# Two sliding-window attention problems on one core: the first loads on one queue, Q weights in halves, second x quarter in two pieces, Q of all blocks ahead of K, first V chain of that quarter unpinned

## The chip, the core and the metric

The kernel runs on one core of a Trainium2 chip. The time is device microseconds of that core for one execution, as a median of several runs. The engines named below are TensorE (PE, with its weight loads as PEld), VectorE (DVE), ScalarE (ACT), GpSimd (POOL) and SyncE (SP), whose queue issues most of the loads.

## The reference

Two independent problems, A and B, each with x of 2048 x 1024, and the results side by side. All inputs are bf16.

```python
def ref(x, wqkv, wo):
    B, S, D = x.shape                      # 1, 2048, 1024
    H = 32; Dh = D // H; W = 256
    qkv = (x @ wqkv).reshape(B, S, 3, H, Dh).transpose(2, 0, 3, 1, 4)
    q, k, v = qkv[0], qkv[1], qkv[2]
    scores = jnp.einsum("bhqd,bhkd->bhqk", q, k) * (Dh ** -0.5)
    idx = jnp.arange(S)
    mask = (idx[:, None] - idx[None, :] >= 0) & (idx[:, None] - idx[None, :] < W)
    p = softmax(jnp.where(mask, scores, -1e9))
    o = jnp.einsum("bhqk,bhkd->bhqd", p, v)
    return o.transpose(0, 2, 1, 3).reshape(B, S, D) @ wo
```

Each query sees the 256 keys up to its own position, so the scores form a band.

## The kernel before

**Tiling.** x is held transposed in quarters of 512 rows (`xT[(problem, quarter)]`, 128 partitions x 8 column tiles x 512). The weights of Q and K come for four heads at a time (a group `g`, 8 groups to a problem, `wqk[g]`), the weights of V for eight heads (`wv[m]`). A *Q or K chain* is eight matmuls of 512 columns that make one group's Q or K for one quarter; a *V chain* is sixteen matmuls of 256 columns for two blocks of 128 rows; an *output chain* is eight matmuls of 512 columns. Each chain ends with a copy out of its bank (`pp`) by ScalarE or VectorE (lines 216 and 218). There are two such banks.

**Sessions.** The band is cut into units of 64 queries by 128 keys; eight units make a score set. A session (`session`, line numbers around 528 to 562) issues the score matmuls of a set, two exponentials on ScalarE and the masks on GpSimd. Between two sessions the kernel's own planner puts in chains: `emit_all` and `forced` take them from a list sorted by the latest session at which they are needed (`late`), each with an earliest session (`early`); `level` works out how much of this work goes in now. Once probabilities times V are due, the chains up to the next session are issued in a split form (four matmuls of 32 columns of weights, line 197, in place of one of 128, line 193).

**The start.** The first quarter of x is loaded as four blocks of 128 rows (`xrow`, line 647) and turned by TensorE (`flip`, eight transposes a block, line 680, then a copy each by ScalarE and VectorE, line 682). `first(which, a)` does Q (`which` 0) or K (1) for one block `a`, eight matmuls of 128 columns. The later quarters come by transposing loads (`load_x`, line 154). The order of the loads on SyncE's queue is that of the code: blocks 0 and 1, K weights, blocks 2 and 3, V weights, second quarter, weights of group 1, third quarter, second V weights, fourth quarter; the Q weights of group 0 are issued by ScalarE. Until data is there TensorE multiplies a blank tile (`keep_warm`, line 667), six times before the first flip and twice after it. On TensorE the order is: flip 0, two blanks, flip 1, Q on block 0, K on block 0, flip 2, Q on block 1, flip 3, K on block 1, Q on blocks 2 and 3, K on blocks 2 and 3, one V chain, then the first session.

Of the kernel before, what the change touches and what calls it, by code (L numbers as in the profile page):

```python
# [10 lines left out]
I32 = mybir.dt.int32  # L11
# [7 lines left out]
P = 128  # L19
# [6 lines left out]
QB = 4  # L26
# [8 lines left out]
NS_MM = 216.0  # L35
# [4 lines left out]
FREE = 10 ** 6  # L40
# [43 lines left out]
def _fast_path(ctx, tc, cfg, problems, outs, consts, certify, osbp, ps_acc, ps_proj, last_stores):  # L84
# [57 lines left out]
    xT, wqk, wv, wo_sb, vts, oTs, qks, pts = {}, {}, {}, {}, {}, {}, {}, {}  # L142
    edges, diags = {}, {}

    top = once.tile([P, 256], I32, name="top")
    nc.vector.memset(top[:], 0)
    blank = top[:].bitcast(BF16)

# [3 lines left out]
    def load_x(pi, k, a=0, n=QB, c0=0, c1=CT):  # L152
        lo, hi = a * P, (a + n) * P
        nc.sync.dma_start_transpose(
            out=xT[(pi, k)][:, c0:c1, lo:hi],
            in_=problems[pi][0][k * 512 + lo:k * 512 + hi, c0 * P:c1 * P])
# [7 lines left out]
    def load_wqk(g, which, queue, lo=0, hi=CT):  # L164
        pi, t = divmod(g, T)
        queue.dma_start(out=wqk[g][:, lo:hi, which, :],
                        in_=wsrc(pi)[:, lo:hi, which, t * P:(t + 1) * P])
# [219 lines left out]
    def landed(*key):  # L387
        return arrival.get(key, 0)
# [18 lines left out]
    for m in range(NM):  # L407
        for b in range(0, NB, 512 // (VG * P)):
            k = b // QB
            early = max(0, landed("x", m * VG // T, k), landed("wv", m))  # L410
            if m > 1:
                early = max(early, pv_time(VG * (m - 1) - 1, min(2 * k + 2, NP - 1)) + 1)
            late = pv_time(VG * m, b // 2) if m or k else 1
            chains.append(_Chain(early, late, v_steps(m, b), dense=True))
# [19 lines left out]
            fixed[d] += NS_PV * (10 if p else 6)  # L434

    current = []

    def start_chain(now, left):
        able = [n for n, c in enumerate(chains) if c.early <= now]
        if not able:  # L440
            return False
        pick = able[0]
        want = whole[0] == (left > 900.0)
        if chains[pick].late > now + 1 and chains[pick].dense != want:
            pick = next((n for n in able if chains[n].dense == want
                         and chains[n].late <= now + REACH), pick)
        current.extend(chains.pop(pick).steps)
        return True

    def run_side():  # L450
# [18 lines left out]
    def emit_all(now, budget):  # L469
        emit(now, budget)  # L470
        second_half()

    def forced(now):
        while any(c.late <= now for c in chains):
            assert current or any(c.early <= now for c in chains), [
                (c.early, c.late, now, c.size) for c in chains if c.late <= now]
            emit(now, sum(ns for ns, _ in current) or chains[0].size)
        if any(c.late <= now + 1 for c in chains):
            emit(now, sum(ns for ns, _ in current))
# [162 lines left out]
    new_wqk(0)  # L642
    new_wv(0)
    xrow = [rows[:, 2 * a:2 * a + 2, :].rearrange("p t n -> p (t n)") for a in range(QB)]
    load_wqk(0, 0, nc.scalar)
    for a in range(QB):
        nc.sync.dma_start(out=xrow[a], in_=problems[0][0][a * P:(a + 1) * P, :])
        if a == 1:
            load_wqk(0, 1, nc.sync)
    load_wv(0, 0, CT, nc.sync)  # L650
    new_x(0, 1)
    load_x(0, 1)
    new_wqk(1)
    for which in range(2):
        load_wqk(1, which, nc.sync)
# [8 lines left out]

    def keep_warm(n):
        for _ in range(n):
            nc.tensor.matmul(warm[:], lhsT=blank[:, 0:P], rhs=blank[:, 0:512], start=True, stop=True)

    keep_warm(6)
    half = CT // 2  # L670
    held = [{}, {}]

# [11 lines left out]
    def first(which, a):  # L684
        for _, f in qk_steps(0, which, 0, a * P, (a + 1) * P, held[which], last=a == QB - 1):
            f()

    with tc.tile_pool(name="ps_flip", bufs=4, space=PSUM) as ps_flip:
        flip(0)
        keep_warm(2)  # L690
        flip(1)
        first(0, 0)
        first(1, 0)
        flip(2)
        first(0, 1)
        flip(3)
        for which, a in ((1, 1), (0, 2), (0, 3), (1, 2), (1, 3)):
            first(which, a)
    emit(0, chains[0].size)

# [2 lines left out]
    for now in range(END):  # L703
        forced(now)
        settle(now)
        whole[0] = not (due and due[0][0] <= now)
        session(now)
        while due and due[0][0] <= now:
            _, pg, pk = due.pop(0)
            finish_norm(1)  # L710
            pv(pg, pk)
        if not whole[0]:
            finish_norm(1)
        if due and due[0][0] == now + 1:
            finish_norm()
        while edges_due and edges_due[0][0] <= now:
            edge(*edges_due.pop(0)[1:])
        emit_all(now, level(now) - fixed[now])
    while edges_due:
        edge(*edges_due.pop(0)[1:])  # L720
    while due:
# [140 lines left out]
@with_exitstack  # L862
def kernel(
    ctx: ExitStack,
    tc: tile.TileContext,
    A_x: bass.AP,
    A_wqkv: bass.AP,
    A_wo: bass.AP,
    B_x: bass.AP,
    B_wqkv: bass.AP,  # L870
    B_wo: bass.AP,
    out: bass.AP,
):
    nc = tc.nc
    S, D = A_x.shape[-2], A_x.shape[-1]
    cfg = _Cfg(S, D)
    problems = [(x.flatten_outer_dims(), wqkv, wo)
                for (x, wqkv, wo) in ((A_x, A_wqkv, A_wo), (B_x, B_wqkv, B_wo))]
    of = out.flatten_outer_dims()
    outs = [of[:, pi * D:(pi + 1) * D] for pi in range(len(problems))]  # L880

    cpool = ctx.enter_context(tc.tile_pool(name="consts", bufs=1))
    ones = cpool.tile([P, 2, 32], BF16, name="ones")
    nc.vector.memset(ones[:], 0.0)
    nc.vector.memset(ones[:, 0, 0:16], 1.0)
    nc.vector.memset(ones[:, 1, 16:32], 1.0)
    ones1 = cpool.tile([P, 1], F32, name="ones1")
    nc.vector.memset(ones1[:], 1.0)
    pm = cpool.tile([P, 1], F32, name="pm")
    okp = cpool.tile([P, 1], F32, name="okp")  # L890
    unsafe_i = cpool.tile([1, 1], I32, name="unsafe_i")
    ident = cpool.tile([P, P], BF16, name="ident")
    nc.gpsimd.memset(ident[:], 0.0)
    nc.gpsimd.affine_select(out=ident[:], in_=ident[:], pattern=[[-1, P]],
                            compare_op=ALU.not_equal, fill=1.0, base=0, channel_multiplier=1)
    consts = {"ones": ones, "ident": ident}

    def reduce_bits(top):
        seen = top[:, 0:8]
        nc.vector.tensor_single_scalar(out=seen, in_=seen, scalar=OUT_OF_RANGE, op=ALU.bitwise_and)  # L900
        nc.vector.tensor_reduce(out=pm[:], in_=seen, axis=AX.X, op=ALU.max)
        nc.vector.tensor_scalar(out=okp[:], in0=pm[:], scalar1=0.5, scalar2=None,
                                op0=ALU.is_lt)

    def decide(pool):
        csum = pool.tile([P, 512], F32, name="pp")
        nc.tensor.matmul(csum[0:1, 0:1], lhsT=ones1[:], rhs=okp[:], start=True, stop=True)
        nc.vector.tensor_scalar(out=unsafe_i[:], in0=csum[0:1, 0:1], scalar1=float(P) - 0.5,
                                scalar2=None, op0=ALU.is_lt)

    last_stores = []
    osbp = ctx.enter_context(tc.tile_pool(name="osb", bufs=4))
    ps_acc = ctx.enter_context(tc.tile_pool(name="ps_acc", bufs=2, space=PSUM))
    ps_proj = ctx.enter_context(tc.tile_pool(name="ps_proj", bufs=2, space=PSUM))
    with tc.manual_schedule():
        with ExitStack() as fctx:
            _fast_path(fctx, tc, cfg, problems, outs, consts, [reduce_bits, decide], osbp, ps_acc,
                       ps_proj, last_stores)

    unsafe = nc.values_load(unsafe_i[0:1, 0:1], min_val=0, max_val=1)  # L920

    with tc.If(unsafe > 0, preferred_fallthrough_block=True) as found:
        with ExitStack() as sctx:
            spool = sctx.enter_context(tc.tile_pool(name="s_consts", bufs=1))
            _make_slow_consts(nc, consts, spool)
            for pi, (x, wqkv, wo) in enumerate(problems):
                with ExitStack() as pctx:
                    _slow_problem(pctx, tc, cfg, x, wqkv, wo, outs[pi], consts)
    with found.Else():
        with tc.manual_schedule():  # L930
            for n, (place, pp, lo, hi) in enumerate(last_stores):
                osb = osbp.tile([P, 512], BF16, name="osb")
                copy = nc.scalar.copy if n % 2 == 0 else nc.vector.tensor_copy
                copy(out=osb[:, lo:hi], in_=pp[:, lo:hi])  # L934
                queue = nc.scalar if n >= 2 else nc.sync
                queue.dma_start(out=place, in_=osb[:, lo:hi])
# [30 lines left out]
```

## Time and profile before

| | |
|---|---|
| median of 3 runs | 599.55 us (598.75 to 599.72) |
| profiled execution | 599.05 us, of which the span is 597.3 us |
| TensorE busy | 582.3 us, 97% of the span |
| ScalarE busy | 402.0 us, 67% |
| GpSimd busy | 365.3 us, 61% |
| VectorE busy | 352.6 us, 59% |
| DMA moved | 35.67 MB, of them 6.37 MB in the first 40 us |

The busy share of an engine is taken over the whole span. What a change in the first microseconds is worth is read from the rows of that stretch: when a load was issued, how long it took to land, and which engine waited for it. In the rows, the time in square brackets is the idle time of the engine just before the row, with what ended it. Ends of matmuls are modelled, so the starts are the safer numbers.

### The profile page before, as it was taken

To read this page: it belongs to the slowest core of one execution; us is meant where nothing else is said; L and a number is where in the kernel's file an instruction comes from. 1 tells how busy PE (TensorE), PEld (TensorE's weight loads), DVE (VectorE), ACT (ScalarE), POOL (GpSimd) and SP (SyncE) were. 2 spreads that over 40 slices of the span, in tenths; PEclk is the share of its full clock that TensorE was granted. 3 is DMA by queue.
4 is the path that set the end of the run, shared out by engine and by line. 5 is a ranking of instruction groups with operands and counts; after the bars stand their busy time and mean duration, and the time that the engine had idled before them with its cause. 6 is when DMAs were issued, how large, how long until landed. Compare 5 with 4: busy or idle time off the path is not lost. (4 is left out here: it accounts for less than half of the span.)

```text
span 597.3 us, 31844 instructions
## 1 busy us (share of the span) xinstructions
PE 582.3 (97%) x14155; PEld 360.2 (60%) x14226; DVE 352.6 (59%) x973; ACT 402.0 (67%) x502; POOL 365.3 (61%) x918
## 2 busy tenths in 40 slices
PE   8999999999999999999999999999999999999997
PEld 6666665666557656566656657665556655555443
DVE  1265766676677776774566656666666656666100
ACT  4667777777877877776567767676676776774332
POOL 0658667777777878765466666666667666665000
PEclk9999999999999999999999999999999999999999
DMA  9915110111024103545011100102030030114122
GB/s 243 181 39 145 39 40 3 40 40 38 4 48 101 39 3 57 109 99 130 10 39 39 38 3 20 42 20 74 3 83 20 24 98 13 55 56 135 64 80 74
DMA packets 86815, 35.67 MB, mean 60 GB/s; under 512 B 65552, under 2 KB 86160, under 8 KB 86672
## 3 DMA queue, kind: packets, MB, share of 16 engines
q1 hardware_dynamic: 85344, 33.18, 22.8%
q8 instruction: 113, 1.85, 1.3%
q10 hardware_dynamic: 1328, 0.39, 0.3%
q14 instruction: 30, 0.25, 0.1%
HBM read 17.83 MB, written 8.39 MB: 44 GB/s over the span
## 5 line engine op out<-in xcount | busy, mean ns | idle before, releaser
L538 ACT ACTIVATE pt<-st 128x1024 bf16<-128x1024 f32 x304 | 299.2, 1025 | 86.7 <-PE st L528 40.6
L549 POOL TENSOR_SCALAR_AFFINE_SELECT diag<-pt 128x256 bf16<-128x256 bf16 x512 | 215.5, 446 | 181.9 <-ACT pt L538 171.1
L562 POOL TENSOR_SCALAR_AFFINE_SELECT pt<-pt 128x512 bf16<-128x512 bf16 (+1 forms) x256 | 155.2, 625 | 0.0
L576 DVE TENSOR_TENSOR both<-diag,pt 128x512 bf16<-128x512 bf16 (+1 forms) x256 | 123.0, 520 | 16.5 <-POOL diag L549 9.6
L193 PE MATMUL pp<-xT,wqk 128*128 128x512 bf16 (+1 forms) x538 | 121.7, 360 | 6.5 <-issue 5.2
L197 PE MATMUL pp<-xT,wqk 128*32 128x512 bf16 x1924 | 114.6, 379 | 0.0
L619 DVE STREAM_TRANSPOSE turned<-acc 128x128 f32<-128x128 f32 x128 | 39.8, 311 | 99.0 <-PE acc L609 99.0
L193 PE MATMUL pp<-wv,xT 128*128 128x256 bf16 x756 | 89.8, 273 | 0.0
L193 PEld LDWEIGHTS <-wqk 128*128 128x128 bf16 x591 | 51.5, 98 | 51.1 <-DMA wqk<-in_A_wqkv_dram 0.2
L193 PEld LDWEIGHTS <-xT 128*128 128x128 bf16 x756 | 72.2, 98 | 14.6
L193 PE MATMUL pp<-wo_sb,oT 128*128 128x512 bf16 x323 | 74.0, 379 | 2.0 <-issue 1.3
L528 PEld LDWEIGHTS <-kT 32*64 32x64 bf16 x3904 | 41.1, 103 | 56.3 <-issue 56.2
L197 PEld LDWEIGHTS <-wqk 128*32 128x32 bf16 x1924 | 48.8, 97 | 39.0
L528 PE MATMUL st<-qT,kT 32*64 32x64 bf16 (+4 forms) x3904 | 65.9, 236 | 0.2 <-issue 0.2
L626 DVE STREAM_TRANSPOSE wide<-inv 128x256 f32<-128x256 f32 x128 | 57.0, 445 | 4.3
L193 PEld LDWEIGHTS <-oT 128*128 128x128 bf16 x357 | 33.9, 98 | 38.4 <-issue 0.2
L627 DVE TENSOR_TENSOR oT<-acc,wide 128x256 bf16<-128x256 f32 x128 | 54.3, 424 | 4.5
L216 ACT CAST osb<-pp 128x512 bf16<-128x512 f32 x49 | 28.7, 586 | 39.5 <-PE pp L193 27.0
L609 PE MATMUL acc<-pt,vt 128*32 128x128 bf16 (+2 forms) x1792 | 48.8, 223 | 0.0
L609 PEld LDWEIGHTS <-vt 128*32 128x32 bf16 x2816 | 43.5, 97 | 7.7 <-issue 0.4
L216 ACT CAST qT<-pp 128x512 bf16<-128x512 f32 x52 | 30.5, 587 | 19.2 <-PE pp L197 10.1
L216 ACT CAST vt<-pp 128x512 bf16<-128x512 f32 x45 | 26.4, 588 | 23.2 <-PE pp L193 12.3
(49 smaller groups left out, 421.8 us busy)
## 6 DMA issues: line engine op xcount, KB each, us to landing
out_dram<-osb SPq DMA_DIRECT2D x63, 128.0 KB, 1.9
wqk<-in_B_wqkv_dram SPq DMA_DIRECT2D x32, 128.0 KB, 2.8
wqk<-in_A_wqkv_dram SPq DMA_DIRECT2D x24, 128.0 KB, 2.9
wo_sb<-in_A_wo_dram SPq DMA_DIRECT2D x16, 128.0 KB, 2.6
wv<-in_B_wqkv_dram SPq DMA_DIRECT2D x16, 128.0 KB, 2.5
wo_sb<-in_B_wo_dram SPq DMA_DIRECT2D x16, 128.0 KB, 2.5
oT<-in_A_x_dram SPq DMA_DIRECT2D x4, 256.0 KB, 4.8
wv<-in_A_wqkv_dram SPq DMA_DIRECT2D x2, 512.0 KB, 6.2
```

Of the source, the lines that this page charges most:

```text
L193: nc.tensor.matmul(out[:, lo:hi], lhsT=lhsT, rhs=rhs, start=start, stop=stop, skip_group_check=True)
L197: nc.tensor.matmul(out[c:c + 32, lo:hi], lhsT=lhsT[:, c:c + 32], rhs=rhs, start=start, stop=stop, tile_position=(0, c), skip_group_check=True)
L216: nc.scalar.copy(out=out, in_=in_)
L528: nc.tensor.matmul(scores[c * HALF:(c + 1) * HALF, r, a * HALF:(a + w_) * HALF], lhsT=kT[rows, keys], rhs=qT[rows, q:q + w_ * HALF], start ...
L538: nc.scalar.activation(out=pt[:, lo:lo + 2, :n * HALF], in_=scores[:, lo:lo + 2, :n * HALF], func=ACT.Exp, bias=-SHIFT, scale=cfg.scale)
L549: nc.gpsimd.affine_select(out=diags[(g, p)][:, :, h, lo:lo + HALF], in_=pt[:, :, a * HALF:(a + 1) * HALF], pattern=[[0, 4], [1, HALF]], co ...
L562: nc.gpsimd.affine_select(out=blk, in_=blk, pattern=[[0, 4], [-1, w_ * HALF]], compare_op=ALU.is_gt, fill=0.0, base=-HALF * (us[a][2] - 3) ...
L576: nc.vector.tensor_tensor(out=both[:, :, h, o:o + w_], in0=dg[:, :, h, o:o + w_], in1=pts[t][:, :, a:a + w_], op=ALU.add)
L609: nc.tensor.matmul(acc[32 * r:32 * r + 32, o:o + w_], lhsT=lhsT, rhs=src[:, r, :], start=(x == 0), stop=(x == len(moves) - 1), tile_positi ...
L619: nc.vector.transpose(out=turned[:], in_=acc[:, 2 * P:3 * P])
L626: nc.vector.transpose(out=wide[:], in_=inv[:].unsqueeze(3).to_broadcast([P, 2, QB, 32]))
L627: nc.vector.tensor_tensor(out=oTs[(pi, k)][:, t, (p % 2) * 256:(p % 2 + 1) * 256], in0=acc[:, 0:256], in1=wide[:], op=ALU.mult)
```

## The change

The Q weights of group 0 move from ScalarE's queue to SyncE's, in two halves of four column tiles, between blocks 1 and 2 of x; the K weights go behind block 3. The second quarter of x is loaded in two pieces of 256 rows. On TensorE, Q of all four blocks now comes ahead of K of all four, the two blank matmuls after flip 0 are gone, and the warm-up is ten blank matmuls of 256 columns in place of six of 512. The blank tile is half as wide; the memsets of the constants `ones` and `ones1` move from VectorE to GpSimd. In the planner, the first V chain of the second quarter may start with session 0, session 0 is followed by at least two chains' worth of work, and a chain that is under way is finished in `forced` once its own latest session has come.

```diff
-    top = once.tile([P, 256], I32, name="top")
+    top = once.tile([P, P], I32, name="top")
...
             early = max(0, landed("x", m * VG // T, k), landed("wv", m))
+            if m == 0 and b == QB:
+                early = 0
...
     current = []
+    current_late = [FREE]
...
-        current.extend(chains.pop(pick).steps)
+        chain = chains.pop(pick)
+        current.extend(chain.steps)
+        current_late[0] = chain.late
         return True
...
     def forced(now):
+        if current and current_late[0] <= now:
+            emit(now, sum(ns for ns, _ in current))
...
-    load_wqk(0, 0, nc.scalar)
     for a in range(QB):
         nc.sync.dma_start(out=xrow[a], in_=problems[0][0][a * P:(a + 1) * P, :])
         if a == 1:
-            load_wqk(0, 1, nc.sync)
+            for c in range(0, CT, 4):
+                load_wqk(0, 0, nc.sync, c, c + 4)
+    load_wqk(0, 1, nc.sync)
     load_wv(0, 0, CT, nc.sync)
     new_x(0, 1)
-    load_x(0, 1)
+    for a in range(0, QB, 2):
+        load_x(0, 1, a, 2)
...
-            nc.tensor.matmul(warm[:], lhsT=blank[:, 0:P], rhs=blank[:, 0:512], start=True, stop=True)
-
-    keep_warm(6)
+            nc.tensor.matmul(warm[:, 0:256], lhsT=blank[:, 0:P], rhs=blank[:], start=True, stop=True)
+
+    keep_warm(10)
...
         flip(0)
-        keep_warm(2)
         flip(1)
         first(0, 0)
-        first(1, 0)
         flip(2)
         first(0, 1)
         flip(3)
-        for which, a in ((1, 1), (0, 2), (0, 3), (1, 2), (1, 3)):
+        for which, a in ((0, 2), (0, 3), (1, 0), (1, 1), (1, 2), (1, 3)):
             first(which, a)
...
-        emit_all(now, level(now) - fixed[now])
+        room = level(now) - fixed[now]
+        emit_all(now, room if now else max(room, 2 * NS_MM * CT))
...
-    nc.vector.memset(ones[:], 0.0)
-    nc.vector.memset(ones[:, 0, 0:16], 1.0)
-    nc.vector.memset(ones[:, 1, 16:32], 1.0)
-    nc.vector.memset(ones1[:], 1.0)
...
+    nc.gpsimd.memset(ones[:], 0.0)
+    nc.gpsimd.memset(ones[:, 0, 0:16], 1.0)
+    nc.gpsimd.memset(ones[:, 1, 16:32], 1.0)
+    nc.gpsimd.memset(ones1[:], 1.0)
```

SyncE's queue at the start of the program, before (`oT` is the tile that holds the rows of x before they are turned; x2 after a row counts it twice in a row):

```order
L647 DMA oT<-in_A_x_dram 128x1024 x2
L166 DMA wqk<-in_A_wqkv_dram 128x8x128
L647 DMA oT<-in_A_x_dram 128x1024 x2
L175 DMA wv<-in_A_wqkv_dram 128x8x256
L154 DMA_TRANSPOSE xT<-in_A_x_dram 128x8x512
```

And after:

```order
L653 DMA oT<-in_A_x_dram 128x1024 x2
L166 DMA wqk<-in_A_wqkv_dram 128x4x128 x2
L653 DMA oT<-in_A_x_dram 128x1024 x2
L166 DMA wqk<-in_A_wqkv_dram 128x8x128
L175 DMA wv<-in_A_wqkv_dram 128x8x256
L154 DMA_TRANSPOSE xT<-in_A_x_dram 128x8x256 x2
```

The whole load of weights ahead of the second pair of blocks was K's; now it is Q's in two halves, K's comes after the pair, and the transposing load is in two.

TensorE, at the end of Q on block 0, before (`pp_179` is Q's bank, `pp_188` K's; in brackets what a row waits for, DMAHW being a load):

```order
L193 LDWEIGHTS wqk_123
L193 MATMUL pp_179<-xT_122,wqk_123 128x128
L193 LDWEIGHTS wqk_123 [waits DMAHW3_49]
L193 MATMUL pp_188<-xT_122,wqk_123 128x128 [waits PE_49]
L193 LDWEIGHTS wqk_123
```

And after (`pp_183` is Q's bank):

```order
L193 LDWEIGHTS wqk_123
L193 MATMUL pp_183<-xT_122,wqk_123 128x128
L689 LDWEIGHTS oT_121 [waits DMAHW4_49]
L689 MATMUL turned_192<-ident_63,oT_121 128x128 [waits PE_49]
L689 LDWEIGHTS oT_121
```

K on block 0 stood there and waited for its weights; now the transposes of block 2 follow at once, and all of K comes after Q on block 3.

ScalarE, which copies the banks out between the exponentials, from the end of the start on, before:

```order
L216 CAST qT<-pp 128x512
L216 CAST kT<-pp 128x512
L216 CAST vt<-pp 128x512
L538 ACTIVATE pt<-st 128x1024 x2
L216 CAST qT<-pp 128x512
L538 ACTIVATE pt<-st 128x1024 x2
```

And after:

```order
L216 CAST qT<-pp 128x512
L216 CAST kT<-pp 128x512
L216 CAST vt<-pp 128x512
L545 ACTIVATE pt<-st 128x1024 x2
L216 CAST vt<-pp 128x512
L216 CAST qT<-pp 128x512
L545 ACTIVATE pt<-st 128x1024 x2
```

One more V chain (`vt`) is finished between the first and the second pair of exponentials, ahead of the Q chain on the second quarter.

## Rows read from the trace of the kernel before

**Rows 1.** The page, part 1: busy us (share of the span) x instructions of TensorE.

```profile
PE 582.3 (97%) x14155; PEld 360.2 (60%) x14226; DVE 352.6 (59%) x973; ACT 402.0 (67%) x502; POOL 365.3 (61%) x918
```

**Rows 2.** Windows: stretch, its length, then busy us of each engine (instructions).

```profile
0.00:15.00 15.00, 13.17 (x156) 9.84 (x156) 2.11 (x9) 6.78 (x10) 0.70 (x6) 1.00 1.02 243
15.00:45.00 30.00, 29.52 (x598) 19.30 (x603) 13.40 (x35) 18.82 (x24) 16.90 (x40) 1.00 0.53 109
```

**Rows 3.** Waits of TensorE over the span: us in total, times, longest.

```profile
PE pp L193 <- issue: 6.5, 41, 0.2
```

**Rows 4.** Timeline of the start, TensorE's matmuls: start us, us, engine, line, out<-in.

```profile
1.31 2.74 PE L667 MATMUL pp<-top 128*128 128x512 bf16 x6 [1.31 <-DVE ones L886]
...
3.85 1.01 PE L680 MATMUL turned<-ident,oT 128*128 128x128 bf16 x8
...
4.69 0.59 PE L667 MATMUL pp<-top 128*128 128x512 bf16 x2
...
5.70 0.62 PE L680 MATMUL turned<-ident,oT 128*128 128x128 bf16 x8 [0.41 <-DMA oT<-in_A_x_dram]
...
8.40 0.61 PE L680 MATMUL turned<-ident,oT 128*128 128x128 bf16 x8
...
8.84 2.40 PE L193 MATMUL pp<-xT,wqk 128*128 128x128 bf16 x40
...
11.08 1.91 PE L193 MATMUL pp<-wv,xT 128*128 128x256 bf16 x16
```

**Rows 5.** Timeline of the start, TensorE's weight loads.

```profile
1.72 0.15 PEld L667 LDWEIGHTS <-top 128*128 128x128 bf16 x1 [0.28 <-issue]
...
5.69 0.45 PEld L680 LDWEIGHTS <-oT 128*128 128x128 bf16 x8 [0.90 <-DMA oT<-in_A_x_dram]
...
6.82 0.45 PEld L193 LDWEIGHTS <-wqk 128*128 128x128 bf16 x8 [0.23 <-DMA wqk<-in_A_wqkv_dram]
7.49 0.45 PEld L680 LDWEIGHTS <-oT 128*128 128x128 bf16 x8 [0.23 <-DMA oT<-in_A_x_dram]
...
15.08 0.98 PEld L193 LDWEIGHTS <-wqk 128*128 128x128 bf16 x6 [0.17 <-DMA xT<-in_A_x_dram]
```

**Rows 6.** Timeline of the start, SyncE's queue: start and length of the issues.

```profile
0.80 0.87 SPq L647 DMA_DIRECT2D oT<-in_A_x_dram  x2
...
2.19 1.05 SPq L647 DMA_DIRECT2D oT<-in_A_x_dram  x2
3.29 0.43 SPq L175 DMA_DIRECT2D wv<-in_A_wqkv_dram  x1
3.76 7.63 SPq L154 DMA_TRANSPOSE xT<-in_A_x_dram  x1
```

**Rows 7.** Loads by narrow windows of issue: KB, us from issue to landing.

```profile
wqk<-in_A_wqkv_dram ACTq DMA_DIRECT2D x1, 256.0 KB, 4.1
oT<-in_A_x_dram SPq DMA_DIRECT2D x1, 256.0 KB, 3.0
...
oT<-in_A_x_dram SPq DMA_DIRECT2D x1, 256.0 KB, 5.3
...
wv<-in_A_wqkv_dram SPq DMA_DIRECT2D x1, 512.0 KB, 6.7
...
xT<-in_A_x_dram SPq DMA_TRANSPOSE x1, 11.3
```

**Rows 8.** Timeline of the start, VectorE: its copy of block 3.

```profile
9.04 0.42 DVE L682 COPY xT<-turned 128x512 bf16<-128x512 bf16 x1 [0.47 <-PE turned L680]
```

**Rows 9.** Transposing loads, line 154: length of the issues, ns min/median/max, starts.

```profile
L154 SPq DMA_TRANSPOSE xT<-in_B_x_dram x32: 1194/1222/2661, 175.8 to 278.5; - x32
L154 SPq DMA_TRANSPOSE xT<-in_A_x_dram x3: 5659/6520/7633, 3.8 to 19.0; - x3
```

**Rows 10.** Groups by form: Q and K chains, wide and split; busy us, mean ns.

```profile
L193 PE MATMUL pp<-xT,wqk 128*128 128x512 bf16 x474 | 117.4, 379 | 6.4 <-issue 5.2 <-PE st L528 0.2
L197 PE MATMUL pp<-xT,wqk 128*32 128x512 bf16 x1924 | 114.6, 379 | 0.0
```

## The prediction

> **What bounds the kernel now.** I read the busy shares first, then the stretches, then who waits for whom, and only then the first 16 us row by row. TensorE is busy 582.3 us of a 597.3 us span [rows 1], and from 15 us on it misses only 0.48 us in 30 us [rows 2]. The longest entry in the list of its waits is 6.5 us put down to "issue", in 41 pieces of 0.2 us at most [rows 3]; next to it only the wait of 1.31 us at the very start is over a microsecond long and has an engine for its cause [rows 4]. So the work after the first stretch is a queue of matmuls with hardly a gap, and a change that reorders this queue can win or lose only what is left in gaps. The one stretch with room is 0 to 15 us, where 1.83 us are idle [rows 2]; there the loads set the pace. The reader is to see three things in rows 4 and 5: the weight loads of TensorE wait 0.90 us for block 1 of x, 0.23 for the K weights and 0.23 for block 2, so each starts as its load lands; from block 2 at 7.49 on nothing waits until the V work starts at 11.08; and the last wait for a load, 0.17 us at 15.08, is for the second quarter of x.
>
> The profiled execution took 599.05 us (597.3 us of span and 1.75 us around it); the median of the three runs is 599.55 and they spread from 598.75 to 599.72. I make the sum as a difference and put it on the median too. A difference of under about 0.2% (1.2 us) is what a measurement of this kernel cannot tell from none.
>
> **Part 1: the order of the loads.** Block 0 of x lands at 0.80 + 3.0 = 3.8, block 1 at 5.69, the K weights at 6.82, block 2 at 2.19 + 5.3 = 7.49, the V weights at 3.29 + 6.7 = 9.99; the Q weights, on ScalarE's queue beside the blocks, take 4.1 us and are there before block 1 [rows 5 to 7]. The time to landing grows from 3.0 to 6.7 us down the queue while the issues follow each other in half a microsecond, so I read these landings as a line of data waiting for the same engines, not as a fixed latency. From this, K cost 6.82 - 5.69 = 1.13 us of the line, and a block of x 7.49 - 6.82 = 0.67. After the change the data ahead of block 2 is blocks 0 and 1 and Q, without K. Whether Q runs beside the blocks or between them, block 2 should land 1.13 us earlier, at about 6.35, block 3 at about 7.0, K at about 8.2, and the V weights at 9.99 as before, since the same bytes are ahead of them.
>
> Bounds of that landing. Optimistic: Q beside block 0 had held it back by half of its 1.13 us; block 0 alone lands at 3.25 and block 2 then at 3.25 + 0.67 + 1.13 + 0.67 = 5.72. Pessimistic: landings are tied to issues. Q in halves puts two issues in front of block 2 where K's one stood; at 0.43 us an issue (the V weights' [rows 6]) block 2 is issued at about 2.6 and by the 5.3 us of its row lands at 7.9. I take 6.35, as the growth of the landing times speaks for the line.
>
> The row for block 0, beside the Q load of the other queue, is 3.0 us from issue to landing, and block 2, four loads later, takes 5.3 [rows 7]. [...]
>
> **Part 2: TensorE up to the first V work.** Before, from block 2's landing: its eight transposes and Q on block 1 from 7.49 to 8.40, block 3's transposes to 8.84, then five groups of eight matmuls (2.24 us, 0.45 each) to 11.08 [rows 4, 5]; 3.59 us in all. After the change K on block 0 stands behind block 2 as well, and the order is: transposes of block 2 and Q on block 1 0.91, transposes of block 3 0.44, Q on blocks 2 and 3 0.90, four groups of K 1.79. That adds 0.45. One wait is new: Q on block 3 needs the copies of block 3, the last of which ends at 9.04 + 0.42 = 9.46 [rows 8], 1.06 us after block 3's transposes start at 8.40; only these transposes and one group lie between now, so 1.06 - 0.44 - 0.45 = 0.17 us. Together 3.59 + 0.45 + 0.17 = 4.21, and the V work starts at 6.35 + 4.21 = 10.56 instead of 11.08: **0.52 us earlier**. With the bounds of part 1 it starts at 9.99 (the V weights hold it there) to 12.1: a gain of 1.09 to a loss of 1.0. The K weights (8.2) are wanted at 8.77 and hold nothing up.
>
> **Part 3: warm-up and memsets.** The warm-up falls from 8 matmuls of 512 columns to 10 of 256, none between the flips. The two removed there took 0.59 us at 4.69 [rows 4], and block 1 came later anyway, so removing them frees nothing. The memset of the blank tile is first on VectorE and half as large; TensorE starts at about 1.1 instead of 1.31, ten matmuls at 0.21 (half of the 0.28 + 0.15 = 0.43 us from one weight load to the next in rows 5) end at about 3.25, and then it waits for block 0. The ones go to GpSimd, which has nothing else to do before the first exponentials. Cost in time: nothing, unless TensorE's clock depends on it (rival 2).
>
> **Part 4: second quarter of x, and the V chain.** Between the first and second score sets the program now has two V chains ahead of the Q chain on the second quarter; the new one needs only the first half of that quarter. The first scores follow the first V chain, at 10.56 + 1.91 = 12.5, take some 0.35 us, and each V chain takes 1.91 [rows 4]; so the first half is wanted at 14.8 and the second at 16.7. Before, the whole landed at 3.76 + 11.3 = 15.06 [rows 6, 7]. It was in line behind the V weights of 9.99, so the first half should be there at about (9.99 + 15.06) / 2 = 12.5. Two pieces cost more issue time: pieces of an eighth take 1.22 us each on the queue against 5.66 us for a whole quarter at best [rows 9], which splits into about 0.6 us a piece and 5.1 us for the data; so 0.6 us more, and the second half lands at 15.1 to 15.7, still ahead of 16.7. The wait of **0.17 us** goes, and the 0.52 us gained ahead of it is not turned into a longer wait there. The third quarter's load begins some 0.6 us later; its first chain stands behind one more V chain of 1.9 us, so its cover grows.
>
> The rest of the order differs up to about the 18th score set and is then the same row for row. The count of wide and split chains moves a little: nine groups fewer of the split 512-column form (114.6 us / 481 groups = 0.238) in favour of the wide one (117.4 us over the 527 in the program = 0.223) [rows 10], 0.13 us less; five V groups more in split form, at the same difference, 0.07 us more. Net **0.06 us** less; its bounds are 0 and 0.13.
>
> **Sum:** 0.52 + 0.17 + 0.06 = 0.75 us less: 599.05 - 0.75 = 598.3 for the profiled execution, 599.55 - 0.75 = **598.8** for the median. That is 0.13%: no change that can be told.
>
> **Rivals.**
> 1. *Landings follow issues.* Then part 1 is at its pessimistic end: V at 12.1, and 1.0 - 0.17 - 0.06 = 0.8 us slower, 600.3. Against it: the landing times that grow from 3.0 to 6.7 us. Chance 0.10.
> 2. *TensorE's clock rises late (the slower side).* [...] After the change there is a gap at 3.25 and another before block 2. A 128-column matmul costs 0.107 at the low level and 0.056 at the high one. If the low level holds over block 1, Q on block 0 (its weights landed by 5.69) ends at 6.55, 0.2 us past block 2's landing, and each further matmul loses 0.05. Up to about 8.0 this is 14 matmuls: 0.7 + 0.2 - 0.75, so 599.7, no change. Slower by 1.2 us needs 35 such matmuls, a low clock up to 10.3; with all 72 up to the V work it is 3.6 + 0.2 - 0.75 = 3.0 us, 602.6. [...] Chance 0.12 for the mild end, 0.05 for the slow one.
> 3. *The second half of the quarter comes late.* It costs from 16.7 on; 1.2 us slower needs a landing past 18.6, 3.5 us later than the whole before. Chance 0.03, 0.02 of it slower.
> 4. *More is won.* With block 2 at 5.72 the V work starts at 9.99 and the gain is 1.09 + 0.17 + 0.13 = 1.39 us, 598.15. Chance 0.12 for over 1.2 us.
>
> **How the numbers follow.** Forecast (a gain of 0.4 to 1.2 us) 0.58; rivals 0.10, 0.17, 0.03, 0.12. Faster 0.12; slower 0.05 + 0.02 = 0.07; within 0.2% the other 0.81. The range runs from rival 4's 598.15 to rival 1's 600.3, each with a little for the spread of runs: 597.9 to 600.4. The slow end of rival 2 and most of rival 3 lie outside.
>
> **What would show it.** Block 2's transposes at 6.2 to 6.6 and the first V matmul at 10.3 to 10.8 bear out parts 1 and 2; block 2 at 7.8 shows rival 1. Eight transposes of block 1 or 2 in about 0.85 us show rival 2. No wait of TensorE on the second quarter bears out part 4, a weight load that waits there for its second half shows rival 3. The forecast is wrong if TensorE's idle time after 15 us changes by more than half a microsecond.

## The result, and the profile after

The changed kernel took 603.07 us (median of six, 602.33 to 604.04) against 599.79 us before (median of six executions of the same comparison, 598.75 to 600.12). The ratio is 1.0061, with an interval of 1.0050 to 1.0072: slower by 3.3 us, outside the forecast range. The profiled execution took 603.45 us, with a span of 601.7 us against 597.3.

The start of the changed kernel, TensorE's matmuls and under them two of its weight loads (as rows 4 and 5):

```profile
1.12 2.31 PE L676 MATMUL pp<-top 128*128 128x256 bf16 x10 [1.12 <-DVE top L146]
...
3.57 1.89 PE L689 MATMUL turned<-ident,oT 128*128 128x128 bf16 x16
...
7.47 1.03 PE L689 MATMUL turned<-ident,oT 128*128 128x128 bf16 x8
...
9.15 1.06 PE L689 MATMUL turned<-ident,oT 128*128 128x128 bf16 x8
...
10.01 3.11 PE L193 MATMUL pp<-xT,wqk 128*128 128x128 bf16 x48
...
12.96 1.91 PE L193 MATMUL pp<-wv,xT 128*128 128x256 bf16 x16
...
6.81 0.34 PEld L193 LDWEIGHTS <-wqk 128*128 128x128 bf16 x4 [1.19 <-DMA wqk<-in_A_wqkv_dram]
7.47 0.77 PEld L689 LDWEIGHTS <-oT 128*128 128x128 bf16 x8 [0.32 <-DMA oT<-in_A_x_dram]
```

The V work starts at 12.96 instead of 11.08 [rows 4]: 1.88 us lost. Block 2 lands at 7.47, where it landed before [rows 5], and the second half of Q only at 6.81. The transposes still take 1.03 and 1.06 us for eight, the slower of the two rates in these traces, where they took 0.62 from block 1 on. The record of the granted clock in the two traces agrees: its first entry, with the full share (1.00), begins at 4.67 us before and only at 10.56 us after.

The rest of the loss comes much later. ScalarE's exponentials of the 19th score set and of the last one, in the kernel before:

```profile
79.38 1.94 ACT L538 ACTIVATE pt<-st 128x1024 bf16<-128x1024 f32 x2 [0.58 <-PE st L528]
...
543.01 1.95 ACT L538 ACTIVATE pt<-st 128x1024 bf16<-128x1024 f32 x2
```

And in the changed one:

```profile
81.50 1.94 ACT L545 ACTIVATE pt<-st 128x1024 bf16<-128x1024 f32 x2 [0.58 <-PE st L535]
...
547.57 1.95 ACT L545 ACTIVATE pt<-st 128x1024 bf16<-128x1024 f32 x2
```

At the 19th set the changed kernel is 2.12 us late, at the last one 4.56 us. Between them both kernels issue the same rows in the same order, and still 2.44 us are lost. Where they go is seen in weight loads of split chains, most of them V chains, that wait for nothing the profile names:

```profile
117.88 0.11 PEld L197 LDWEIGHTS <-xT 128*32 128x32 bf16 x6 [0.71 <-issue]
...
130.88 0.10 PEld L197 LDWEIGHTS <-xT 128*32 128x32 bf16 x3 [0.32 <-issue]
...
289.06 1.31 PEld L197 LDWEIGHTS <-xT 128*32 128x32 bf16 x49 [0.81 <-issue]
...
378.76 0.86 PEld L197 LDWEIGHTS <-xT 128*32 128x32 bf16 x32 [1.10 <-issue]
```

In the list of waits these and smaller ones are one line, in the changed kernel and before:

```profile
PEld L197 <- issue: 5.6, 11, 1.1
...
PEld L197 <- issue: 1.8, 3, 1.2
```

Seven of the eleven stand in split V chains, two in split Q or K chains and two in split output chains. Two of the three before are:

```profile
285.02 1.54 PEld L197 LDWEIGHTS <-xT 128*32 128x32 bf16 x59 [1.19 <-issue]
...
374.18 1.10 PEld L197 LDWEIGHTS <-xT 128*32 128x32 bf16 x42 [0.39 <-issue]
```

One trap: TensorE's busy share rose to 99%, and the 6.5 us of "issue" in 41 pieces [rows 3] are absent from this trace. They are back in other kernels' traces (6.3 us in 40 pieces in the first experiment, which is slower than before). Traces that have the entry hold some 70 fewer matmuls than weight loads (14155 and 14226 before [rows 1]); the changed kernel's has 14216 of both. So the entry goes with missing records and was no time to be won.

### The profile page after: what moved, and what is told of

Its sections match the earlier page's. It is cut to its first block, busy times and chain, and to the rows that moved or that the text cites. A ratio compares the mean times of both kernels' runs of the same rounds, so it can differ in the third digit from the quotient of the medians.

```text
span 601.7 us, 31898 instructions
## 1 busy us (share of the span) xinstructions
PE 593.3 (99%) x14216; PEld 363.8 (60%) x14216; DVE 350.9 (58%) x967; ACT 403.1 (67%) x504; POOL 364.5 (61%) x922
## 4 chain that ended last, share of the span: by engine, by line
PE 98%; DMA 1%; issue 0%; SPq 0%; DVE 0%; DVEq 0%
PE pp L193 47%; PE pp L197 28%; PE acc L616 13%; PE st L535 9%; DMA oT<-in_A_x_dram 1%; PE turned L689 0%; PE acc L193 0%; SPq L166 0%; SPq L653 0%; DVE osb L942 0%; DVE unsafe_i L916 0%; PE pp L915 0%; DVEq L942 0%
## 5 line engine op out<-in xcount | busy, mean ns | idle before, releaser
L193 PE MATMUL pp<-xT,wqk 128*128 128x512 bf16 (+1 forms) x600 | 133.1, 366 | 0.9 <-DMA wqk<-in_A_wqkv_dram 0.9
L193 PEld LDWEIGHTS <-wqk 128*128 128x128 bf16 x600 | 53.6, 99 | 53.1 <-DMA wqk<-in_A_wqkv_dram 1.2
L193 PE MATMUL pp<-wo_sb,oT 128*128 128x512 bf16 x341 | 76.7, 379 | 0.2 <-DVE unsafe_i L916 0.2
```

The lines of the kernel that those rows point to most:

```text
L193: nc.tensor.matmul(out[:, lo:hi], lhsT=lhsT, rhs=rhs, start=start, stop=stop, skip_group_check=True)
```

## The experiments

In all but the last, which is a single execution, the kernel before had medians of 599.8 to 600.0 us beside them, and the ratios are to it. Where a blank matmul of one column is added it is of this form, into the scratch bank of the warm-up:

```diff
+    for _ in range(10):
+        nc.tensor.matmul(warm[:, 0:1], lhsT=blank[:, 0:P], rhs=blank[:, 0:1], start=True, stop=True)
```

**The warm-up undone (e1).** The changed kernel with

```diff
-            nc.tensor.matmul(warm[:, 0:256], lhsT=blank[:, 0:P], rhs=blank[:], start=True, stop=True)
-    keep_warm(10)
+            nc.tensor.matmul(warm[:], lhsT=blank[:, 0:P], rhs=blank[:, 0:512], start=True, stop=True)
+    keep_warm(6)
...
         flip(0)
+        keep_warm(2)
```

> The changed kernel with the warm-up of before (six blank matmuls of 512 columns, two more after flip 0). Theory A: in the changed kernel TensorE ran at the low level up to about 10.5 us, because the shorter warm-up let it idle, and that is most of the 1.9 us by which its V work started later (12.96 against 11.08). Then eight transposes take 0.45 us again from block 1 on, the V work starts at about 11.7 (block 2's landing at 7.47 plus 4.21), and the time falls by about 1.3 us, to 601.8. Rival B: the loads set the pace and the clock follows them; then the V work stays at 12.5 to 13.0 and the time at 603.

602.29 us, ratio 1.0034 (1.0021 to 1.0046). Block 1's transposes, block 2's, and the V work:

```profile
4.77 0.61 PE L689 MATMUL turned<-ident,oT 128*128 128x128 bf16 x8
...
7.41 0.62 PE L689 MATMUL turned<-ident,oT 128*128 128x128 bf16 x8 [0.27 <-DMA oT<-in_A_x_dram]
...
11.60 1.91 PE L193 MATMUL pp<-wv,xT 128*128 128x256 bf16 x16
```

The V work is 1.36 us sooner, as theory A said, and the record of the granted clock begins at 3.99 us instead of 10.56. Block 2 lands no earlier (7.41 against 7.47). The median falls by 0.8 of the 1.3 us expected.

**Q back on ScalarE's queue (e2).**

```diff
+    load_wqk(0, 0, nc.scalar)
     for a in range(QB):
...
-            for c in range(0, CT, 4):
-                load_wqk(0, 0, nc.sync, c, c + 4)
```

> The changed kernel with the Q weights whole on ScalarE's queue again, K still behind block 3. Theory B: the two halves of Q on SyncE's own queue held up what stands behind them (second half landed at 6.81, block 2 at 7.47 as before although K was gone from ahead of it). Then Q lands by about 5 us, block 2 at about 6.35, the wait of 0.9 us for Q goes, and with no such gap the clock may rise sooner: V work at 10.6 to 12.3 instead of 12.96, 0.7 to 2.4 us less. Rival A, the warm-up alone: block 2 comes earlier but the transposes still take 0.85 us up to about 10.5, V work at 12.4 or later, 0.6 us less at most.

603.90 us, ratio 1.0060 (1.0043 to 1.0077), but in two groups: 601.28 and 601.67, and four at 603.9 to 604.6. The profiled one is the 601.28: its V work starts at 10.87, block 2's transposes at 6.68 without a wait (0.61 us for eight), and its clock record begins at 4.85. The four longer ones have no trace. By the 1.95 us of e8 below, a low rate that lasts longer would cost most of the difference of 2.2 to 3.3 us; this is an estimate, and no run shows it.

**The planner's edits undone (e3).**

```diff
-            if m == 0 and b == QB:
-                early = 0
...
-        if current and current_late[0] <= now:
-            emit(now, sum(ns for ns, _ in current))
...
-        room = level(now) - fixed[now]
-        emit_all(now, room if now else max(room, 2 * NS_MM * CT))
+        emit_all(now, level(now) - fixed[now])
```

> The changed kernel without its three edits in the planner, so that the first V chain of the second quarter stands where it stood. Theory C: the planner's edits only reorder work that TensorE does anyway and cost nothing by themselves; the time stays within 0.6 us of 603.1. Rival D: the later part of the loss (2.4 us between the 18th score set and the end, where the order of both kernels is the same) comes with the edits, through the shift of TensorE's instruction stream by 20 rows or the other split chains; then the time falls by 1 to 2.4 us.

601.42 us, ratio 1.0020 (1.0008 to 1.0032): 1.65 us back, though the V work still starts at 12.94. Theory C falls: the planner's edits carry about half of the loss.

**The same place in the stream (e4).** Ten blanks of one column behind `keep_warm(10)`.

> The changed kernel with ten more blank matmuls of one column after the warm-up, so that from the 18th score set on every row stands at the same place of TensorE's stream as in the kernel before. Theory E: the stalls put down to issue in the split chains (weight loads of line 197: 5.6 us in 11 pieces in the changed kernel against 1.8 us in 3 before) depend on where in the stream a row stands; then they fall back to about 2 us and the time by 1.5 to 2.4 us, to 601 or 601.5. Rival F: they fall at random, or follow the loads in flight; then they stay between 2 and 6 us at other places and the time does not move by more than 0.6 us.

601.09 us, ratio 1.0016 (1.0006 to 1.0026): 2.0 us back from adding work, with 3.3 us of these stalls instead of 5.6. That is more than theory E's 2 us of stalls, but rival F, which allowed such a sum, did not allow the fall of the time. The V work came at 12.61 in its trace, so some 0.35 of it may be the start's.

**The same in the kernel before (e5).** Ten blanks behind the two after flip 0.

> The kernel before with ten more blank matmuls of one column after the two behind flip 0, where TensorE waits for block 1 anyway, so that all that follows stands 20 rows later in its stream. Theory E (stalls by place in the stream): the start stays as it was within 0.1 us, the V work at 11.1, and the later part changes by stalls at other sessions; the 20 rows go the other way than the changed kernel's, so the sign is not fixed: 0 to 2.5 us more, with stalls put down to issue of 3 to 6 us instead of 1.8. Rival F (at random or by the loads): the same stalls and the same time within 0.4 us.

598.69 us, ratio 0.9979 (0.9968 to 0.9990): faster than both kernels by adding ten blanks. Theory E had expected 0 to 2.5 us more: that the place matters was right, the direction was missed. The V work starts at 10.99, within 0.1 us of before, and no stall of line 197 is left in its trace; one of 0.86 us now stands in a score set (line 528, at 234.9 us).

**The planner's edits alone (e6).** The kernel before with e3's lines put in.

> The kernel before with the three planner edits alone, the loads, the warm-up and the order of Q and K as before; its stream after the 18th score set stands 24 rows earlier. Theory E with a front without loss: V work at 11.1, the wait of 0.17 us for the second quarter stays or goes, and after the 18th score set 1.4 to 2.4 us more than before, with the stalls of the changed kernel at the same sessions (28 and 104 by 0.4 to 0.8 us each): 601 to 602. Rival: the later loss of the changed kernel hangs on its loads or its start; then 599.6, as the kernel before.

603.21 us, ratio 1.0051 (1.0034 to 1.0067): as much as the whole loss of the changed kernel, with the old loads and the old warm-up. Not all of it is the later stretch: in its trace the V work starts at 11.46 (0.38 late) and a weight load near the end waits 0.7 us for the output weights. From the 19th score set to the last it takes 2.5 us more than before. Its stalls:

```profile
116.18 0.10 PEld L197 LDWEIGHTS <-xT 128*32 128x32 bf16 x4 [0.98 <-issue]
...
129.48 0.09 PEld L197 LDWEIGHTS <-xT 128*32 128x32 bf16 x1 [0.63 <-issue]
...
287.65 1.21 PEld L197 LDWEIGHTS <-xT 128*32 128x32 bf16 x47 [0.79 <-issue]
...
377.26 0.77 PEld L197 LDWEIGHTS <-xT 128*32 128x32 bf16 x30 [0.99 <-issue]
```

Here the reader can count. A weight load and its matmul are two rows of the program. The stall near 117 us leaves 6 weight loads before the next score set in the changed kernel and 4 here; that score set begins at row 5325 of TensorE's stream there and at 5321 here. So the stall stands at row 5325 - 12 = 5321 - 8 = **5313** in both. The one near 130 us is row **6081** in both. The one near 287 us leaves 59, 49 and 47 loads of its row in the kernel before, the changed one and this one. The 10 and 12 loads by which these differ are the 20 and 24 rows by which the streams differ there, so it too stands at one row in all three. Counted through the traces, with one row for each of the few wait rows in TensorE's list, that row is **14529**, which is 5313 + 36 times 256 (the 14589 and 19129 in the expectation of e9 do not agree with this count, by which the second is 19137). And the first five of the changed kernel's, rows 2497, 4033, 5313, 6081 and 6849, differ by 6, 5, 3 and 3 times 256.

**All three parts mended (e7).** The edits of e1 and e2 together, and twelve blanks behind the two after flip 0.

> The changed kernel with Q whole on ScalarE's queue, the warm-up of before, and twelve blank matmuls of one column after those behind flip 0, so that the later rows stand where they stood before. Theories A, B and E together: clock at the higher level from about 4.5, block 2 by 6.6, V work at 10.6 to 10.9 in all runs, stalls of 2 to 3.5 us: 599.0 to 600.0, at or a little under the kernel before. If the shift of the stream is not what costs, the later part still loses 1.4 to 2.4 us against before: 601 to 602.

600.15 us, ratio 1.0010 (1.0000 to 1.0021). Block 2's transposes and the V work:

```profile
6.36 0.62 PE L689 MATMUL turned<-ident,oT 128*128 128x128 bf16 x8
...
10.55 1.91 PE L193 MATMUL pp<-wv,xT 128*128 128x256 bf16 x16
```

The start is won (10.55), but it is given back up to the 19th score set: that set comes 0.04 us earlier than before, where the start was 0.53 us earlier. Of the 0.49 us, 0.43 are one stall of the same kind, at 42.8 us in a split V chain.

**The warm-up alone (e8).** The kernel before with the changed warm-up.

> The kernel before with the changed warm-up alone (ten blank matmuls of 256 columns, none behind flip 0, a blank tile half as wide); its stream shifts by 4 rows. Theory A: the clock rises late in some or all runs, since TensorE now waits from about 4.8 to 5.7 for block 1; where it does, each eight transposes or matmuls take 0.85 us up to about 10 and the V work starts at 12.3 to 13.2: 601 to 602, with a spread of 2 us between runs. Rival B (the loads alone): V work at 11.1 and 599.8 within 0.4 us.

601.78 us, ratio 1.0023 (1.0011 to 1.0034): five runs at 600.15 to 600.73, seven at 601.74 to 602.75. In the profiled execution the first eight transposes of block 1 and the V work are

```profile
5.81 1.03 PE L680 MATMUL turned<-ident,oT 128*128 128x128 bf16 x8 [0.87 <-DMA oT<-in_A_x_dram]
...
13.03 1.91 PE L193 MATMUL pp<-wv,xT 128*128 128x256 bf16 x16
```

so the warm-up alone costs 1.95 us at the start of this execution, whose clock record begins only at 10.65 us, and 1.9 us in the median.

**The planner's edits, rows back in place (e9).** e6 with twelve blanks behind the two after flip 0.

> The kernel before with the three planner edits (603.2 us, 3.35 over before) and twelve blank matmuls of one column behind flip 0, where TensorE waits; after the 18th score set every row then stands where it stood before. Theory E: the stalls at rows 5313, 6081 and 6849 of TensorE's stream now fall outside the split V chains and go, those at 14589 and 19129 are those of before; 599.6 to 600.5. If the planner's order itself costs (its other split chains, one V chain more ahead), the time stays at 602.5 to 603.5.

600.66 us, ratio 1.0014 (1.0003 to 1.0026). Twelve blanks take 2.55 of the 3.35 us back. The stalls at rows 5313 and 6081 are gone, but not because these rows left the split V chains, as expected: 16 and 13 loads of such chains still follow them. What differs is that 20 and 27 split loads stand directly ahead of them, where e6 has 32 and 39. The third that was to go, at row 6849, stays (0.60 us). The one at 14529 and the one after it are back where the kernel before had them, with 59 and 42 loads left:

```profile
285.86 1.54 PEld L197 LDWEIGHTS <-xT 128*32 128x32 bf16 x59 [0.78 <-issue]
...
375.26 1.10 PEld L197 LDWEIGHTS <-xT 128*32 128x32 bf16 x42 [0.66 <-issue]
```

**Twenty rows further (e10).** e7 with 22 blanks.

> As the run with Q on ScalarE's queue, the warm-up of before and 12 blank matmuls of one column (600.15 us), but with 22 of them: the later rows stand 20 rows later than before, where the padded kernel before had its 598.7 us. Theory E: V work at 10.55 to 10.7, the stalls of the padded kernel, 598.0 to 598.9, under both kernels. Against it: the stretch up to the 18th score set has another order and its own stalls, up to 0.7 us; then 599.0 to 599.6.

599.76 us, ratio 0.9997 (0.9988 to 1.0006). Short of the hope: the longer row of blanks ends late (V work at 11.20 in its trace). From the 19th score set to the last it takes 462.59 us against 463.63 before, about 1 us less; in e5 it is 463.23.

**The loads and the order of Q and K alone (e11).** The kernel before with the changed loads and firsts.

> The kernel before with the loads and the order of Q and K of the changed kernel alone (Q in halves on SyncE's queue, K behind block 3, second quarter in two pieces, Q of all blocks ahead of K), warm-up and planner as before; no row after the start moves. Theory B: the second half of Q lands at 6.4 to 6.8, block 2 at 7.3 to 7.5, the clock rises at about 4.5, the V work starts at 11.6, and the second quarter does not hold it up: 0.5 us more than before, 600.2 to 600.6. If the loads in line were as good as beside each other, as predicted: V work at 10.6, 599.3.

600.38 us, ratio 1.0006 (0.9997 to 1.0016): V work at 11.91, 0.83 late. Theory B's sign, and no gain; the median alone could not be told from no change.

**Q in one piece on the same queue (e12).** e1 with `load_wqk(0, 0, nc.sync)` in place of the two halves.

> The changed kernel with the warm-up of before and Q whole, in one load, on SyncE's queue between blocks 1 and 2. If the halving made Q slow in line (2.7 us from block 1's landing to that of its second half), Q now lands about 1.1 us after block 1, at 5.3, block 2 at 6.4, and the V work starts at 10.6. If it is the one queue, on which the 256-byte rows of Q run with nothing beside them, Q lands at 6.4 or later, block 2 at 7.2 to 7.5, and the V work starts at 11.4 to 11.7, as with the halves.

One execution, read for its start alone:

```profile
6.68 0.45 PEld L193 LDWEIGHTS <-wqk 128*128 128x128 bf16 x8 [1.44 <-DMA wqk<-in_A_wqkv_dram]
7.36 0.45 PEld L688 LDWEIGHTS <-oT 128*128 128x128 bf16 x8 [0.23 <-DMA oT<-in_A_x_dram]
```

Q lands at 6.6, block 2 at 7.36, V work at 11.55: as with the halves. It is the one queue, not the halving. It is not the issue of block 2 either: here it is issued at 2.19, in the changed kernel at 2.74, and it lands only 0.1 us sooner.

## Why the prediction was wrong, point by point

**What bounds the kernel** was right: TensorE's queue bounds it, and the loss is gaps in that queue. But the last sentence of it, that a reordering can win or lose "only what is left in gaps", was taken to mean that nothing is lost. New gaps can be opened, and were.

**Part 1 failed at the step "whether Q runs beside the blocks or between them".** Beside the blocks, on ScalarE's queue, Q and blocks 0 and 1 were through at 5.7; in line on one queue block 1 lands at 4.15 (1.25 + 2.9) in the changed kernel but Q 2.4 to 2.7 us later (e1, e12 and the changed kernel), against the 1.13 us that K's row had given. The gain of 1.13 us that K's move makes is there when Q stays on its own queue: block 2 goes at 6.36 in e7, against 6.35 in the prediction. The two kernels' windows from 4 to 6 us show less moved in the changed kernel, 223 and 193 GB/s against 321 and 276 before (the last number of each row, changed kernel first):

```profile
4.00:5.00 1.00, 1.00 (x12) 1.00 (x11) 0.35 (x1) 0.58 (x1) 0.00 (x0) 1.00 0.85 223
5.00:6.00 1.00, 0.89 (x9) 0.62 (x6) 0.49 (x2) 0.58 (x1) 0.00 (x0) 1.00 0.69 193
...
4.00:5.00 1.00, 1.00 (x11) 0.79 (x8) 0.11 (x1) 0.48 (x1) 0.00 (x0) 1.00 1.12 321
5.00:6.00 1.00, 0.59 (x8) 0.31 (x7) 0.32 (x1) 0.10 (x1) 0.00 (x0) 1.00 1.31 276
```

Rival 1 named block 2 at 7.9 from tied issues. It landed at 7.47, and e12, where an issue 0.55 us earlier brings 0.1 us, speaks against its mechanism. Between e12 and e7 the second queue saves 1.0 us, of which at most 0.47 is block 2's earlier issue (1.72 against 2.19).

**Part 2** was right in its working. From block 2's landing to the V work it counted 4.21 us; e1 has 11.60 - 7.41 = 4.19, e7 10.55 - 6.36 = 4.19.

**Part 3 failed**: the warm-up cost 1.36 us at the start of the changed kernel (e1) and 1.95 alone (e8). This is rival 2, given 0.17 with 0.05 for its slow end. Its condition was a low clock up to 10.3; in the changed kernel the transposes at 9.15 still run at the low rate and the clock record begins at 10.56. Rival 2's two costs of a 128-column matmul, 0.107 and 0.056, are borne out: from 8.30 to 9.15 us in the changed kernel eight take 0.85 us, 0.106 each, and from 7.86 to 8.31 in e1 eight take 0.45, 0.056 each. No run shows by itself what brings the change of rate. The two blanks between the flips, costed at nothing because "block 1 came later anyway", were what filled that wait: with them eight transposes take 0.61 us at 4.77 (e1), without them TensorE sits idle from 4.9 to 5.8 and eight take 1.03 (e8). e2's profiled start had the short warm-up too and its clock record begins at 4.85, so the point of the change also differs between executions. Over all the traces, the clock record of the nine with the long warm-up begins at 3.96 to 5.61 us, and block 2's eight transposes take 0.61 or 0.62; of the five with the short one, it begins at 9.86 to 10.72 in four, with 1.03 to 1.06 for these transposes, and at 4.85 in e2, with 0.61. The memsets have no run of their own; the first blank matmul started at 1.12, as forecast.

**Part 4** came out on the loads, with luck: TensorE did not wait for the second quarter, though its first half lands only at 5.00 + 10.2 = 15.2 and not at 12.5. The forecast wanted it at 14.8; it was not missed because the V work came 2.4 us later than forecast. Part 4 failed in the sentence that called the rest "the same row for row" and priced it at 0.06 us. The same rows 20 places earlier in TensorE's stream took 2.44 us more, which is the prediction's own sign of being wrong, idle time after 15 us that changes by more than half a microsecond. This was in no rival, and it is the larger part of the loss and as much of the error as the start: the planner's edits alone cost 3.35 us (e6), and blanks take 2.55 of it back (e9). In all the traces the stretch from the 19th score set to the last, 12080 weight loads and their matmuls in the same order, goes by where these rows stand:

| rows of the stretch, against before | traces | 19th to last set, us |
|---|---|---|
| 20 or 24 earlier | changed kernel, e1, e2, e6, e12 | 466.0 to 466.6 |
| the same or 4 later | before, e3, e4, e7, e8, e9, e11 | 463.6 to 465.6 |
| 20 later | e5, e10 | 462.6 and 463.2 |

The groups do not overlap, and e4, e7 and e9, which have the planner's edits and their rows put back in place, stand with the kernel before: the place is the cause. The trace of the kernel before is the shortest of its group, so 2.44 us is a large reading: from the middle of one group to the middle of the next it is some 1.7 us.

The parts do not add: 3.35 (planner), 1.9 (warm-up) and 0.4 (loads, within the noise) alone, 3.3 together. Part of it is plain: late weights and a low clock overlap at the start (1.95 and 0.83 alone, 1.88 together), and each kernel's rows stand at other places (20, 24 or 4 rows off). The rest was not followed further.

## What to carry to other kernels

When an edit adds or drops instructions on the engine that bounds the kernel, everything after it moves in that engine's stream; here 20 or 24 rows went with some 1.7 us of 600. Before a change as small as this one (0.6%) is credited or blamed, it should be timed with the stream padded back (a few blank matmuls in a wait) and by one or two other paddings. Filler in a wait for data can be worth its place even if the data comes later anyway: without the longer warm-up the V work started 1.36 us (changed kernel against e1) and 1.95 us (e8 against before) later. And Q's load cost less beside the others, on a queue of its own, than in line ahead of what is waited for (block 2 at 6.36 in e7 and at 7.36 in e12); that is worth trying elsewhere.

## What the runs showed of the hardware

**The stalls of split weight loads stand a multiple of 256 rows apart.** The fourteen traces list 71 idle pieces of 0.15 to 1.5 us before split weight loads (line 197) that nothing named ends. Counted as in e6, every one stands within a row of 2497 plus a multiple of 256. Most are in split V chains, whose rows go by faster than those of the other chains (64 weight loads and 64 matmuls in some 1.7 us, where a split Q or K chain has 32 of each in 1.9), some in split Q, K and output chains, a few larger ones in score sets or wide chains (0.86 us in e5). Not every such row stalls. Take the idle pieces of over 0.15 us at these rows out of the stretch from the 19th set to the last, and 460.6 to 461.4 us are left in all fourteen, where the stretch itself runs from 462.6 to 466.6; so these pieces are nearly all of what differs. What TensorE waits for at these rows no line of a trace names: the place of the stalls and their length were measured, their cause was not shown. How long a given stall is was not settled: at one row, 14529, it goes from 0.7 to 1.5 us in twelve traces, and none is there in e5 and e10. More split loads directly ahead of the row seem to make a stall likelier (rows 5313 and 6081: none with 20 and 27 of them in e9, 0.98 and 0.63 us with 32 and 39 in e6); DMA loads of weights had been issued 3.2 to 5.2 us ahead of the two longest of the kernel before and of the changed one, but no run took them away.

**Block 2 landed sooner with Q's load beside it than in line.** The same bytes stand ahead of it, but it lands at 6.36 with Q on ScalarE's queue (e7) and at 7.36 with Q whole in line (e12). At most 0.47 us of this is its later issue; what the rest comes from was not shown. Rates do not settle why: the windows above have less moved in line, but e12, also in line, moved 205 GB/s from 4 to 5 us and 339 from 5 to 6.
